# Every second ReLU of the first FFN batch on VectorE: linear attention, Fourier mixing and an FFN on one Trainium2 core

## The chip, the cores and the metric

The kernel runs on one core of one Trainium2 chip. The metric is the device time of one launch in microseconds (us), as the median of several runs. The kernel before takes 438.59 us (three runs, 438.15 to 439.4).

## The reference

Eight batches of 8 heads, 576 rows and 64 columns pass through a linear attention whose feature map has 2 x 128 features; the result, as 576 x 512 per batch, is mixed by the real part of a 2-D Fourier transform, normalised, and put through a two-layer FFN.

```python
def phi(x):
    proj = np.einsum('bhsd,df->bhsf', x, w_phi)
    proj = proj - np.max(np.abs(proj), axis=-1, keepdims=True)
    return np.concatenate([np.exp(proj), np.exp(-proj)], axis=-1)
q_p, k_p = (phi(q), phi(k))
kv = np.einsum('bhsf,bhsd->bhfd', k_p, v)
z = np.sum(k_p, axis=2)
num = np.einsum('bhsf,bhfd->bhsd', q_p, kv)
den = np.einsum('bhsf,bhf->bhs', q_p, z)[..., None] + 1e-06
attn = num / den                      # then (batch, 576, 512) = x
...
mixed = np.real(np.fft.fft(np.fft.fft(x, axis=1), axis=2))
u = x + mixed
mu = np.mean(u, axis=-1, keepdims=True)
var = np.mean((u - mu) ** 2, axis=-1, keepdims=True)
un = (u - mu) / np.sqrt(var + 1e-06)
ch = np.maximum(un @ w_ch1, 0.0) @ w_ch2       # 512 -> 2048 -> 512
out = u + ch
```

The ReLU in question is `np.maximum(..., 0.0)`, with 2048 hidden features per row.

## The kernel before

The work of a batch is split into generators, called streams, and each call of `step` runs one of them up to its next `yield`. The string `PLAN` (lines 23 to 37) is the order, written out by hand, in which the steps of all streams and batches are issued; line 1344 walks through it. A step issues its instructions to all the engines it uses, and each engine then runs its own instructions in that order. Instructions of different engines are tied together by semaphores where one needs what another made.

The streams that matter here are these:

- T, `steps` of `features` (lines 624 to 632), projects keys and queries on TensorE into PSUM tiles `psk`, `psh`, `ph` (pool `pj`, two buffers) and takes their exponentials on ScalarE: `KPp` and `KPn` (L502), `QPHP` and `QPHN` (L611, L586).
- P, `maxima`, projects the queries again into tiles `psq` and takes their row maxima on VectorE, `MQ` (L560, L538). In batches 0 and 1 each step takes two `psq` tiles from the pool `pb`.
- R, `kmax`, takes the row maxima of `psk` on VectorE, `MK` (L516). S, `scaled`, makes `VCn` and `VCp` from them, first a small exponential on ScalarE (L466), then the product on GpSimd (L471).
- M, `mixing`, first multiplies features and values (`kv`, L892 and L896, copied by ScalarE as `kvh`, L900), then combines each head (`pn_`, L992; `tg`, `cb`, `rd` on VectorE, L999 to L1006; `X` on GpSimd, L1007), then does the Fourier transform.
- N, `normalise`, subtracts the row mean (`nm` on VectorE, L1131 and L1136; `UN` on ScalarE, L1145) and, in batch 0, transposes on TensorE (`put`, L1160) with a copy to `UT` (L1164 on VectorE, L1166 on ScalarE). U, `scales`, takes the statistics on VectorE (L1175, L1176).
- F, `forward`, is the FFN. `hidden` makes 16 groups (hh = 0 to 15) of four matmuls each into a tile `psf` (L1220) and applies the ReLU to it on ScalarE into `HT` (L1224). In batch 0 it runs twice in a row, for the columns 0 to 256 and for 256 to 576, before `output` (L1231, then L1237 on VectorE) begins; each group is one step of F. Below, h0 to h15 are the groups with 256 columns and g0 to g15 those with 320.

The tiles `psf`, `psq`, `put`, `pu`, `pm`, `px` and `pso` share the pool `pb`, which has three buffers in PSUM. They are handed out in turn, so a tile's first matmul waits until the tile that was asked for three places earlier has been read out by its reader. While batch 0 is in `hidden`, the plan runs the features, maxima and `kv` of batch 1 between its groups.

Of the kernel before, what the change touches and what calls it, by code (L numbers as in the profile page):

```python
# [9 lines left out]
AT = mybir.ActivationFunctionType  # L10
# [30 lines left out]
def kernel(  # L41
# [10 lines left out]
    nc = tc.nc  # L52
# [1145 lines left out]
    def store(b, U, c):  # L1198
        if c == 1:
            for a in range(8):  # L1200
                nc.sync.dma_start(
                    out=out[b, 225 - 32 * a:257 - 32 * a, :].rearrange("(r j) n -> r j n", j=2),
                    in_=U[16 * a:16 * a + 16, 0:2, 0:C],
                )
        elif c in (2, 3):
            rows_ = out[b, 320:576, :].rearrange("(a r j) n -> a r j n", r=16, j=2)
            nc.sync.dma_start(out=rows_[:, ::-1, 3 - c, :], in_=U[:, c, 0:C])
        elif c == 4:
            nc.sync.dma_start(out=out[b, 257:320, :], in_=U[1:64, 4, 0:C])
            nc.sync.dma_start(out=out[b, 0:1, :], in_=U[0:1, 4, 0:C])  # L1210

    def forward(b):
        U, UT = turned_u[b]
        HT = fpool.tile([128, NHH, S], BF16, tag="HT", name="HT")

        def hidden(lo, hi):
            for hh in range(NHH):
                ps = pb.tile([128, hi - lo], F32, tag="pb", name="psf")
                for cc in range(NCC):
                    nc.tensor.matmul(  # L1220
                        ps[:], lhsT=W1b[:, cc, 128 * hh:128 * hh + 128], rhs=UT[:, cc, lo:hi],
                        start=(cc == 0), stop=(cc == NCC - 1),
                    )
                nc.scalar.activation(out=HT[:, hh, lo:hi], in_=ps[:], func=AT.Relu)  # L1224
                yield

        def output(c):
            at = PLACE[c]
            po = pb.tile([128, C], F32, tag="pb", name="pso")
            for hh in range(NHH):  # L1230
                nc.tensor.matmul(  # L1231
                    po[:], lhsT=HT[:, hh, at:at + 128], rhs=W2b[:, hh, :],
                    start=(hh == 0), stop=(hh == NHH - 1),
                )
                if hh % 2 and hh < NHH - 1:
                    yield
            nc.vector.scalar_tensor_tensor(  # L1237
                out=U[:, c, 0:C], in0=po[:], scalar=scale_of[b, c], in1=U[:, c, 0:C],
                op0=ALU.mult, op1=ALU.add,
            )  # L1240
            store(b, U, c)
            yield

        yield from hidden(0, 256)
        if b == 0:
            yield from hidden(256, S)
        yield from output(0)
        yield from output(2)
        if b > 0:
            yield from hidden(256, S)  # L1250
        yield from output(1)
        yield from output(3)
        po = pb.tile([128, C], F32, tag="pb", name="pso")
        for hh in range(NHH):
            g = 64 * (hh % 2)
            nc.tensor.matmul(
                po[g:g + 64, :], lhsT=HT[:, hh, 512:576], rhs=W2b[:, hh, :],
                start=(hh < 2), stop=(hh >= NHH - 2),
            )
            if hh % 4 == 3 and hh < NHH - 1:  # L1260
                yield
        for g in (0, 64):
            nc.vector.scalar_tensor_tensor(
                out=U[0:64, 4, 0:C], in0=po[g:g + 64, :], scalar=scale_of[b, 4][0:64],
                in1=U[0:64, 4, 0:C], op0=ALU.mult, op1=ALU.add,
            )
        store(b, U, 4)
        yield
# [109 lines left out]
```

## Time and profile before

The profiled execution has a span of 436.2 us; the run it was taken from gave 438.0 us. The runs without a profile have their median at 438.59 us.

| engine | busy us | share of the span |
|---|---|---|
| TensorE (PE) | 407.8 | 93% |
| VectorE (DVE) | 339.6 | 78% |
| ScalarE (ACT) | 308.3 | 71% |
| GpSimd (POOL) | 208.6 | 48% |

The granted TensorE clock is 0.99 of full speed. A busy TensorE is not one at its peak, since the ends of its matmuls are modelled. The shares are averages over the whole span. The FFN's first layer of batch 0 lies at 53 to 84 us, and there the shares are others; the tables by stretch (columns: busy us of PE, of its weight loads PEld, of DVE, of ACT, of POOL, with instruction counts; then granted clock, DMA share and GB/s) and the chain of work that ended last (columns: start us, us, what) show that part by itself.

### The profile page before, as it was taken

The page shows a single profiled execution, that of the slowest core. Times are in us where ns is not written, and L with a number is a line of the kernel's source. Part 1 is how long each engine was busy: PE and PEld are TensorE (multiplying, and loading weights), DVE is VectorE, ACT ScalarE, POOL GpSimd, SP SyncE. Part 2 cuts the span into 40 slices and gives each one's busy share as a digit, 9 for nine tenths or more (in the row PEclk, how much of TensorE's full clock was granted, in tenths as well). Part 3 has the DMA queues.
Part 4 walks back from the last instruction along what each step waited for, and adds up shares of the span by engine and source line. Part 5 has one row for each costly group of instructions (what it writes and reads, how often), then busy time and mean ns, then how long its engine had stood idle before and what let it go on. Part 6 is the DMA issues. An engine that isn't in the chain of part 4 may idle for free.

```text
span 436.2 us, 10470 instructions
## 1 busy us (share of the span) xinstructions
PE 407.8 (93%) x4110; PEld 255.4 (59%) x4110; DVE 339.6 (78%) x720; ACT 308.3 (71%) x661; POOL 208.6 (48%) x269
## 2 busy tenths in 40 slices
PE   8888898989899999999899899999999999999993
PEld 3564476643675548565666458565766467656561
DVE  6989875899959985998679985898889885965302
ACT  2986999655985798498847788588957886346350
POOL 7982568646545094636645445823652542300100
PEclk9899999999999999999999999999999999999998
DMA  8899995976469357493779467693743050104304
GB/s 223 164 204 147 158 142 60 167 88 108 85 71 141 55 99 128 82 152 54 134 88 127 43 92 100 105 143 61 128 89 59 16 109 20 26 0 77 66 23 84
DMA packets 108626, 42.70 MB, mean 98 GB/s; under 512 B 82849, under 2 KB 103457, under 8 KB 108577
## 3 DMA queue, kind: packets, MB, share of 16 engines
q0 software_dynamic: 45936, 16.60, 34.2%
q1 hardware_dynamic: 62481, 25.38, 31.0%
q8 instruction: 32, 0.52, 0.5%
q14 instruction: 17, 0.14, 0.1%
q10 hardware_dynamic: 160, 0.07, 0.1%
HBM read 36.77 MB, written 9.44 MB: 106 GB/s over the span
## 4 chain that ended last, share of the span: by engine, by line
PE 48%; DVE 28%; ACT 14%; POOL 3%; DMA 3%; issue 2%; DVEq 0%; POOLq 0%; ACTq 0%; SPq 0%
PE psf L1220 22%; PE pso L1231 12%; DVE cb L1004 4%; DVE tg L999 3%; DMA UT<-UN 3%; DVE MK L516 2%; DVE R L908 2%; DVE X L1095 2%; PE kv L892 2%; PE psD L1050 2%; ACT HT L1224 2%; DVE X L1237 2%; DVE st L1175 2%; ACT KPn L502 2%; ACT QPHN L611 1%
## 5 line engine op out<-in xcount | busy, mean ns | idle before, releaser
L1220 PE MATMUL psf<-UT,W1b 128*128 128x320 bf16 (+1 forms) x1024 | 142.2, 286 | 3.8 <-DMA UT<-UN 3.4
L1231 PE MATMUL pso<-W2b,HT 128*128 128x512 bf16 x512 | 125.7, 379 | 0.0
L1224 ACT ACTIVATE HT<-psf 128x256 bf16<-128x256 f32 (+1 forms) x256 | 100.0, 416 | 33.7 <-PE psf L1220 26.5
L1220 PEld LDWEIGHTS <-W1b 128*128 128x128 bf16 x1024 | 94.6, 98 | 35.0 <-issue 10.0
L1231 PEld LDWEIGHTS <-HT 128*128 128x128 bf16 x512 | 45.8, 98 | 44.2 <-issue 1.6
L1007 POOL TENSOR_TENSOR X<-cb,rd 128x320 f32<-128x320 f32 x56 | 41.2, 735 | 59.8 <-DVE rd L1006 44.5
L471 POOL TENSOR_TENSOR VCn<-VS,VCn 128x512 bf16<-128x512 bf16 x28 | 29.7, 1062 | 36.2 <-ACT VCn L466 30.4
L502 ACT ACTIVATE KPp<-psk 128x1024 bf16<-128x1024 f32 x28 | 28.8, 1030 | 22.3 <-PE psk L496 22.2
L560 DVE TENSOR_REDUCE MQ<-psq 128x8 f32<-128x1024 f32 (+1 forms) x32 | 34.3, 1084 | 9.3 <-PE psq L552 9.1
L1237 DVE SCALAR_TENSOR_TENSOR X<-pso,rs,X 128x512 f32<-128x512 f32 x32 | 23.6, 738 | 22.8 <-PE pso L1231 22.7
L502 ACT ACTIVATE KPn<-psk 128x1024 bf16<-128x1024 f32 x28 | 28.6, 1022 | 13.9 <-DVE MK L516 13.6
L516 DVE TENSOR_REDUCE MK<-psk 128x8 f32<-128x1024 f32 x28 | 33.9, 1212 | 0.2
L1095 DVE TENSOR_TENSOR X<-pu,X 128x512 f32<-128x512 f32 (+3 forms) x49 | 23.6, 530 | 11.8 <-PE pu L1105 11.7
L1152 ACT ACTIVATE UN<-X,nm 128x512 bf16<-128x512 f32 (+1 forms) x35 | 25.0, 724 | 10.7 <-DVE nm L1151 9.7
L456 POOL TENSOR_TENSOR V4N<-VS,V4N 64x256 bf16<-64x256 bf16 x14 | 8.9, 638 | 48.1 <-ACT V4N L452 34.5
L611 ACT ACTIVATE QPHP<-psh 128x1024 bf16<-128x1024 f32 x28 | 28.8, 1028 | 2.3 <-PE psh L602 1.9
L471 POOL TENSOR_TENSOR VCp<-VS,VCp 128x512 bf16<-128x512 bf16 x28 | 29.7, 1061 | 0.0
L611 ACT ACTIVATE QPHN<-psh 128x1024 bf16<-128x1024 f32 x28 | 28.7, 1027 | 0.0
L1175 DVE BATCH_NORM_STATS2 st<-X 128x6 f32<-128x512 f32 (+1 forms) x40 | 27.2, 680 | 0.0
L1191 POOL TENSOR_TENSOR rs<-VE,mhalf 128x5 f32<-128x5 f32 (+1 forms) x9 | 10.2, 1139 | 33.2 <-DVE VE L1190 33.2
L992 PEld LDWEIGHTS <-QPHP 128*128 128x128 bf16 x280 | 20.8, 99 | 5.6 <-DVE cb L1004 2.1
L289 POOL DMA_DIRECT2D QS<-in_q_dram x28 | 23.1, 827 | 0.0
(457 smaller groups left out, 803.0 us busy)
## 6 DMA issues: line engine op xcount, KB each, us to landing
out_dram<-X SPq DMA_DIRECT2D x16, 256.0 KB
out_dram<-X SPq DMA_DIRECT2D x64, 64.0 KB
KS<-in_k_dram POOLq DMA_DIRECT2D x7, 512.0 KB, 7.6
QS<-in_q_dram POOLq DMA_DIRECT2D x14, 256.0 KB, 8.0
VS<-in_v_dram POOLq DMA_DIRECT2D x14, 256.0 KB, 6.1
W1b<-in_moe_w_ch_dram POOLq DMA_DIRECT2D x1, 2048.0 KB, 18.9
W2b<-in_moe_w_ch_dram POOLq DMA_DIRECT2D x1, 2048.0 KB, 15.4
W2b<-in_k_dram SPq DMA_DIRECT2D x2, 512.0 KB
```

The lines of the kernel that those rows point to most:

```text
L471: nc.gpsimd.tensor_tensor(out=VC[:, hs, :, 0:D], in0=values[b][0][:, hs, :].rearrange("p h (j d) -> p h j d", d=D), in1=VC[:, hs, :, D:D + ...
L502: nc.scalar.activation(out=KP[:, hs, :, :].rearrange("p e (jp jj) f -> p jj (e jp) f", jj=2), in_=psk[:], func=AT.Exp, scale=sgn,)
L516: nc.vector.tensor_reduce(out=MK[:, 2 * pr:2 * pr + 2, :].rearrange("p e (jp jj) -> p jj (e jp)", jj=2), in_=tiles[pr][:], axis=AX.X, op=A ...
L560: nc.vector.tensor_reduce(out=o, in_=i[:], axis=AX.X, op=ALU.max, apply_absolute_value=True)
L611: nc.scalar.activation(out=o, in_=psh[:], func=AT.Exp, scale=sgn)
L1007: nc.gpsimd.tensor_tensor(out=X[:, :, D * h:D * h + D], in0=cb[:, :, 0:D], in1=rd[:].to_broadcast([128, 5, D]), op=ALU.mult,)
L1095: nc.vector.tensor_tensor(out=to, in0=more, in1=to, op=ALU.add)
L1175: nc.vector.bn_stats(out=st[0:M, :], in_=X[0:M, c, 0:C])
L1220: nc.tensor.matmul(ps[:], lhsT=W1b[:, cc, 128 * hh:128 * hh + 128], rhs=UT[:, cc, lo:hi], start=(cc == 0), stop=(cc == NCC - 1),)
L1224: nc.scalar.activation(out=HT[:, hh, lo:hi], in_=ps[:], func=AT.Relu)
L1231: nc.tensor.matmul(po[:], lhsT=HT[:, hh, at:at + 128], rhs=W2b[:, hh, :], start=(hh == 0), stop=(hh == NHH - 1),)
L1237: nc.vector.scalar_tensor_tensor(out=U[:, c, 0:C], in0=po[:], scalar=scale_of[b, c], in1=U[:, c, 0:C], op0=ALU.mult, op1=ALU.add,)
```

## The change

In batch 0, the groups with odd hh have their ReLU done by VectorE, as a maximum with 0, in place of ScalarE. This concerns h1, h3, ... h15 and g1, g3, ... g15, 16 of the 32 ReLUs of batch 0. The other batches, the matmuls and the plan are as before. Each moved instruction keeps its place in the order of issue, between what the plan issues before and after it to the engine that it now runs on. Lines after the edit are numbered three higher: the ScalarE ReLU becomes L1227, the VectorE one is L1225.

```diff
@@ hidden @@
-                nc.scalar.activation(out=HT[:, hh, lo:hi], in_=ps[:], func=AT.Relu)
+                if b == 0 and hh % 2:
+                    nc.vector.tensor_scalar_max(out=HT[:, hh, lo:hi], in0=ps[:], scalar1=0.0)
+                else:
+                    nc.scalar.activation(out=HT[:, hh, lo:hi], in_=ps[:], func=AT.Relu)
                 yield
```

## The prediction

> **What bounds the kernel now.** The ReLUs of batch 0 lie in one stretch, so I read the chain of waits for that stretch first (start us, us, what).
>
> ```profile
> 53.94 0.72 ACT UN L1145
> 54.66 0.82 ACT HT L1224 x3
> 55.48 0.51 ACT UT L1166
> ...
> 73.67 0.33 ACT HT L1224
> 74.00 0.17 ACT kvh L900
> 74.17 0.04 issue
> 74.21 0.62 PE pt L568 x4
> ...
> 78.06 0.33 PE pn__1491 L992 x10
> 78.39 0.02 issue
> 78.41 0.51 DVE tg L999
> ...
> 83.87 0.57 DVE R L908
> ```
>
> From 53.94 to 74.17 every link is on ACT. Then PE leads for 4 us, and from 78.41 DVE leads; the chain of the next stretch stays on DVE until 104.56. So the 32 ReLUs fall into three parts: 16 (h) and six (g0 to g5) on an ACT-bound path, four (g6 to g9) around the PE part, and the last six in a DVE-bound part. How full each engine is comes from the stretches:
>
> ```profile
> 58.00:62.00 4.00, 3.76 (x59) 3.00 (x58) 3.85 (x8) 4.00 (x10) 4.00 (x6) 1.00 1.07 123
> 62.00:66.00 4.00, 3.75 (x51) 2.66 (x45) 3.17 (x6) 4.00 (x11) 1.54 (x2) 1.00 0.84 87
> ...
> 78.00:82.00 4.00, 4.00 (x59) 2.96 (x57) 3.24 (x10) 3.16 (x8) 3.20 (x4) 1.00 1.55 161
> ```
>
> ACT is at 4.00 of 4.00, but DVE (the third count) is not free: 3.85 of 4 at 58 to 62. What room DVE has is in its timeline, where the idle time before an instruction stands in brackets:
>
> ```profile
> 58.08 0.68 DVE L1090 SCALAR_TENSOR_TENSOR X<-pu,X 64x512 f32<-64x512 f32 x1 [1.20 <-PE pu L1105]
> 62.38 1.29 DVE L560 TENSOR_REDUCE MQ<-psq 128x4 f32<-128x512 f32 x2 [0.42 <-PE psq L552]
> 67.84 1.28 DVE L538 TENSOR_REDUCE MQ<-psq 64x4 f32<-64x512 f32 x2 [0.52 <-PE psq L532]
> 76.55 0.50 DVE L999 TENSOR_TENSOR tg<-pn__1450,E 128x325 f32<-128x325 f32 x1 [3.78 <-ACT HT L1224]
> 78.41 0.50 DVE L999 TENSOR_TENSOR tg<-pn__1491,E 128x325 f32<-128x325 f32 x1 [0.56 <-PE pn__1491 L992]
> ```
>
> With 0.31 and 0.35 in two rows not shown, DVE is idle for 1.20 + 0.42 + 0.31 + 0.52 + 0.35 + 3.78 + 0.56 = 7.14 us up to 83.87, and over half of that is one gap at 72.8 to 76.55, late in the stretch.
>
> **What the Trainium skill says.** "VectorE: DVE Perf Modes", section "Why PSUM operands drop a tier": an fp32 operand in PSUM leaves VectorE at one element a cycle. The trace agrees: the bf16 copy of 320 fp32 elements out of PSUM took 491 ns, 512 elements from SBUF only 486 ns.
>
> ```profile
> L1056 DVE CAST DT<-psD 128x320 bf16<-128x320 f32 x1 | 0.5, 491 | 1.8 <-ACT DT L1055 1.8
> L1140 DVE TENSOR_SCALAR UN<-X,nm 128x512 bf16<-128x512 f32 x1 | 0.5, 486 | 0.0
> ```
>
> "PSUM — Partial Sum Buffer", section "Engine vs sequencer instructions": the queues of ScalarE and VectorE are strictly first in, first out, so a waiting ReLU holds everything behind it. In the trace each engine's instructions start in program order. The same page, "PSUM bank collisions raise a hardware error": two engines may not touch one bank at once, so readers of one tile are ordered. That fits L516 and L502, which both only read `psk`: ACT waited for DVE there ten times, 13.6 us. Hence a late `MK` can hold ACT and the reverse.
>
> **The change part by part.**
>
> *Off ACT.* Back to back, a 256-column ReLU takes 0.27 us of the chain (three took 0.82) and a 320-column one 0.33. Up to 74.17, eight of the first and three of the second go: 8 x 0.27 + 3 x 0.33 = 3.2 us of ACT work. That is the most this part can give.
>
> *On DVE.* The trace has no ReLU on DVE. Nearest is the L1056 copy, 0.49 us for 320 elements; with the 512-element copy of L380 at 0.685 us the slope is 0.194 / 192 = 1.0 ns an element, so 256 elements come to 0.43. Instructions in a row overlap by 0.08 to 0.09 us (two L560 of 0.68 took 1.28), so the queue pays 0.34 and 0.40: 8 x 0.34 + 8 x 0.40 = 5.9 us. The skill's price (the first page, section "The TRN2 errata — SBUF-src ops pay a fixed extra latency per instruction", 120 cycles plus one per element at 0.96 GHz) gives 0.39 and 0.46, 0.03 us less each, so 5.4 us with the same overlap. I take 5.9 and keep 5.4 as the lower end.
>
> *The two together.* If every idle moment of DVE could be used, DVE would reach its instruction of 83.87 by 7.14 - 5.9 = 1.2 us sooner (1.7 with the lower price). The room bounds the gain at 1.2 to 1.7 us, whatever ACT saves.
>
> *What it reaches in order.* I followed the queues by hand from 53 us, with durations and waits of the trace, the DVE ReLUs at their new places and the three `pb` buffers handed out as before. From PE to the reader I count 0.04 us (the tenth 320-column group ended at 78.92, its ReLU began at 78.96), from the reader's visible end to PE 0.03 (ReLU end 54.95, `put` 54.98). The delays against before:
> - h1 stands between the two `MK` of 52.80; its matmuls end at 54.07, so it costs 0.16 of wait and 0.34. h3 stands behind the second `MK`, 0.30 before its matmuls end at 55.86, and costs 0.30 and 0.34. All that follows on DVE is 1.15 late, `nm` too, on which ACT's `UN` (56.65) waits: ACT, two ReLUs lighter, starts it 0.60 late.
> - The wait of 1.20 before 58.08 takes up most of h5 and of that delay; X is 0.2 late, h7 follows, and the `MQ` pair of 59.54 starts at 60.1 (+0.55). Its two tiles are the buffers that h9 and h10 wait for, so PE comes 0.5 late to h10, the next `kv` and `psk`, and ACT's KPp of 62.16 starts at 62.7.
> - h9 precedes the next `MK` and `MQ`; h11 and h13 the `MK` of 64.41. h13's matmuls end at 65.3, and this `MK` ends at 66.9, not 65.6. ACT's VCn (65.85 in the chain), which reads it, starts at 66.95 (+1.1), though ACT has done seven ReLUs fewer by then; it idles.
> - h15 and g1 come before the L538 pair (67.84), which starts at 69.3 (+1.4); g3 keeps this. Its tiles hold up g2 and g3 on PE, and through `psq` and `kv` ACT's QPHN of 69.58 (+1.2).
> - g5 lies in the 3.78 gap and costs DVE nothing, and ACT is a ReLU shorter: `kvh` of 73.78, `pt` of 74.21 and `tg` of 76.55 come 1.1 late.
> - g7 is ready behind the first `rd` and fills the 0.56 wait in part; with g9 behind it the second `tg` is 1.27 late. g11, g13, g15 lie in the DVE-bound part and add 3 x 0.40 = 1.2: R of 83.87 is 2.5 late.
>
> From there the chain is DVE's to 104.56 and no second path is shortened, so 2.5 us go to the end. Against the profiled span: 436.2 + 2.5 = 438.7; the runs without a profile have their median at 438.59, 2.4 above that span, so 438.59 + 2.5 = 441.1 us. The matmuls, DMA issues and GpSimd's work are neither more nor fewer and keep their order.
>
> **The rivals.** A change within 0.3% (1.3 us) can't be told from none here.
> 1. *ACT's relief wins.* For it: ACT is full for 20 us and leads the chain, and PE was held by it (put at 54.98, `pt` at 74.21). If the waits that I place in front of h3, h9 and h13 close up because PE and ACT both run earlier, DVE's idle time is used and the room decides: 438.59 - 1.2 to 1.7 = 436.9 to 437.4. Against it: over half of the room is one gap at 72.8, which ReLUs queued before it fill only by being late.
> 2. *No difference.* The first part gains or loses under 1 us where I have a loss of 1.1, and the 1.4 us behind 76.55 takes the gain away: -1.0 + 1.4 = +0.4, 439.0 us. For it: my path has many links, each good to about 0.05 us.
> 3. *Pile-up.* The idle time doesn't take up any ReLU, as each of them waits for PE behind a maximum that PE's next buffer waits for: 438.59 + 5.9 = 444.5 at the most; half-way from my forecast, 442.8. Against it: the gap at 72.8 hides at least g5.
>
> **How the numbers follow.** My forecast, 441.1 us with its own range 439.9 to 442.6, has 0.5; no difference (437.3 to 439.9) 0.27; ACT's relief 0.12, of which the part over 0.3% needs the lower price too; pile-up 0.11. Slower is forecast and pile-up, 0.61; within 0.3% 0.27; faster 0.12, rounded up for what my path may have wrong in sign. The range of 437.6 to 443.2 leaves out about one in ten on either side.
>
> **What would show it.** Right: L1225 in 16 rows at 0.43 and 0.49 us, with idle time in front of several ascribed to `psf`; ACT below full at 62 to 74; VCn of 65.85 and the L538 of 67.84 later by about 1; the first `tg` after 76.55 and R of 83.87 later by 1 and 2.5; from there the same distance to the end. Wrong: the first `tg` before 76; or ReLUs at under 0.35 us; or a delay at 84 that is smaller at the end. If L516 and L560 keep their old times up to 68, the coupling through the three buffers is what I have wrong.

## The result and the profile after

The changed kernel takes 443.32 us (median of four runs, 442.36 to 444.64) where the kernel before takes 438.47 beside it: 4.85 us more, a ratio of 1.0106 with a 95% interval of 1.0066 to 1.0146. The forecast was 441.1, so the sign was right, the loss was about twice the 2.5 us that I had worked out, and the time lies 0.1 us beyond the upper end of the range.

The profiled execution has a span of 440.5 us, 4.3 more than before. As the clearest measure of the stretch I take the time on VectorE from the first of the two `MK` maxima ahead of the ReLUs (L516, at 52.80 before) to the start of `R` (L908, at 83.78 in the timeline of before; the chain, which puts a start where the instruction ahead has ended, says 83.87). It was 83.78 - 52.80 = 30.98 us. In the timeline of VectorE of the changed kernel (start us, us, instruction, idle time in front in brackets) it is 88.01 - 52.00 = 36.01, 5.03 us more:

```profile
52.00 1.21 DVE L516 TENSOR_REDUCE MK<-psk 128x8 f32<-128x1024 f32 x1
...
55.56 1.07 DVE L234 TENSOR_SCALAR TURN<-gs,blk 128x128 f32<-128x128 f32 x1
56.55 0.14 DVE L230 TENSOR_SCALAR blk<-pc_i 128x1 f32<-128x1 int32 x1
56.73 0.92 DVE L234 TENSOR_SCALAR TURN<-gs,blk 128x128 f32<-128x128 f32 x1
57.57 0.20 DVE L1131 TENSOR_SCALAR nm<-sm 128x1 f32<-128x1 f32 x1
...
62.67 0.42 DVE L1225 TENSOR_SCALAR HT<-psf 128x256 bf16<-128x256 f32 x1 [0.80 <-PE psf L1220]
...
79.44 0.50 DVE L999 TENSOR_TENSOR tg<-pn__1450,E 128x325 f32<-128x325 f32 x1 [2.47 <-ACT HT L1227]
...
88.01 1.67 DVE L908 TENSOR_TENSOR R<-X 128x512 f32<-128x512 f32 x2
```

This execution reached the stretch 0.80 us sooner than the one before (52.00 and 52.80). The two run together up to 15.2 us and are 0.68 us apart at an `MK` maximum (L843, at 22.42 and 23.10); between these points TensorE's granted clock is 0.55 and 0.59 in before (16 to 18 and 18 to 20 us), and 1.00 in the changed kernel. From `R` to the end the two are alike: 440.5 - 88.0 = 352.5 and 436.2 - 83.8 = 352.4. So the loss arises in the stretch, and 5.03 - 0.80 + 0.1 = 4.3 is the difference of the spans.

Two things in it were not in my working. The first is TURN, two tables of 128 x 128 numbers that VectorE makes once in this stretch (L234), and that nothing reads before the `pt` matmuls (L568, at 74.21 in before). Its two instructions took 1.07 and 0.92 us; before, they took 0.29 each (first fence below, VectorE of before). What differs is what GpSimd does meanwhile (second and third fence, GpSimd of before and of after):

```profile
55.27 0.29 DVE L234 TENSOR_SCALAR TURN<-gs,blk 128x128 f32<-128x128 f32 x1
...
55.65 0.29 DVE L234 TENSOR_SCALAR TURN<-gs,blk 128x128 f32<-128x128 f32 x1
```

```profile
53.81 0.62 POOL L456 TENSOR_TENSOR V4P<-VS,V4P 64x256 bf16<-64x256 bf16 x1
56.57 1.06 POOL L471 TENSOR_TENSOR VCn<-VS,VCn 128x512 bf16<-128x512 bf16 x1 [2.13 <-issue]
```

```profile
55.49 1.06 POOL L471 TENSOR_TENSOR VCn<-VS,VCn 128x512 bf16<-128x512 bf16 x1 [1.85 <-issue]
56.51 1.06 POOL L471 TENSOR_TENSOR VCp<-VS,VCp 128x512 bf16<-128x512 bf16 x1
```

Before, TURN ran while GpSimd was idle (54.4 to 56.57). After, h1 and h3 hold it back, and it starts at 55.56, just behind the start of VCn at 55.49. Both sides moved: counted from the first L516, TURN starts 1.09 us later (3.56 for 2.47), and VCn 0.28 sooner (3.49 for 3.77), as ScalarE, without h1, comes sooner to the exponential that it needs (L466). Each TURN ends 0.08 us behind the product that it started beside (56.63 and 56.55, 57.65 and 57.57). The Trainium skill's page "SBUF — State Buffer", section "Who interferes with whom", says that VectorE in its two-port modes and GpSimd share a pair of ports, and that the one that issues first keeps the other out for the whole instruction. The rows above agree with that, as far as they go: that TURN runs in such a mode is not shown. It took 0.78 + 0.63 = 1.41 us more than before.

The second thing is TensorE's clock (stretches of the changed kernel; columns as in the prediction, the clock is the third number from the right):

```profile
57.20:59.20 2.00, 0.95 (x8) 0.63 (x8) 1.97 (x6) 1.39 (x3) 2.00 (x4) 1.00 1.22 196
59.20:61.20 2.00, 1.56 (x22) 1.23 (x22) 1.97 (x8) 2.00 (x4) 1.99 (x3) 0.76 1.17 95
61.20:63.20 2.00, 2.00 (x11) 1.44 (x10) 1.20 (x4) 1.00 (x3) 1.27 (x2) 0.50 1.26 119
63.20:65.20 2.00, 1.82 (x32) 1.39 (x31) 1.72 (x3) 1.56 (x3) 0.00 (x0) 0.89 0.31 46
```

Before, the clock was 1.00 through 50 to 64 us. Here it falls to 0.50, some 2 us behind a stretch in which PE waited for buffers (busy 0.95 of 2.00). The matmuls of h8 to h10 are drawn out (2.75 us for 1.68), ScalarE is at 1.00 of 2.00, and h9's ReLU waits 0.80 us for them. Such a drop is not new: the profile of before has one at 16 to 20 us, ahead of the stretch.

The ReLUs themselves cost what I took, 0.41 to 0.43 us for 256 columns and 0.45 to 0.49 for 320 (the answer for L1225, min/median/max in ns):

```profile
L1225 DVE TENSOR_SCALAR HT<-psf x16: 408/438/492, 53.4 to 87.6; 128x256 bf16<-128x256 f32 x8, 128x320 bf16<-128x320 f32 x8
```

### The profile page after: what moved, and what is told of

Its sections match the earlier page's. It is cut to its first block, busy times and chain, and to the rows that moved or that the text cites. A ratio compares the mean times of both kernels' runs of the same rounds, so it can differ in the third digit from the quotient of the medians.

```text
span 440.5 us, 10444 instructions
## 1 busy us (share of the span) xinstructions
PE 406.3 (92%) x4080; PEld 255.9 (58%) x4110; DVE 346.9 (79%) x736; ACT 304.5 (69%) x645; POOL 208.8 (47%) x269
## 4 chain that ended last, share of the span: by engine, by line
PE 50%; DVE 33%; ACT 10%; DMA 3%; issue 2%; POOL 1%; DVEq 0%; ACTq 0%; POOLq 0%; SPq 0%
PE psf L1220 22%; PE pso L1234 11%; DVE cb L1004 4%; DVE tg L999 3%; DMA UT<-UN 3%; DVE MK L516 3%; PE idle L1312 2%; PE kv L892 2%; DVE X L1095 2%; DVE st L1175 2%; DVE R L908 2%; PE psD L1050 2%; DVE X L1240 2%; DVE MQ L560 2%; DVE rd L1006 1%
## 5 line engine op out<-in xcount | busy, mean ns | idle before, releaser
L1234 PE MATMUL pso<-W2b,HT 128*128 128x512 bf16 x482 | 121.7, 379 | 1.6 <-issue 0.5
L1227 ACT ACTIVATE HT<-psf 128x256 bf16<-128x256 f32 (+1 forms) x240 | 93.9, 413 | 35.9 <-PE psf L1220 28.8
L516 DVE TENSOR_REDUCE MK<-psk 128x8 f32<-128x1024 f32 x28 | 33.9, 1212 | 0.0
```

The lines of the kernel that those rows point to most:

```text
L516: nc.vector.tensor_reduce(out=MK[:, 2 * pr:2 * pr + 2, :].rearrange("p e (jp jj) -> p jj (e jp)", jj=2), in_=tiles[pr][:], axis=AX.X, op=A ...
L1234: nc.tensor.matmul(po[:], lhsT=HT[:, hh, at:at + 128], rhs=W2b[:, hh, :], start=(hh == 0), stop=(hh == NHH - 1),)
```

## The experiments

The theory after the result: three parts, namely the queue order of the forecast, the collision of TURN with GpSimd, and the clock. Its first rival is plain load: each ReLU adds its 0.34 or 0.40 us to VectorE's queue, and the late TURN fills a wait that would be there anyway. "Stretch" below is the time from the first L516 to L908 as above, of the profiled execution; medians are compared with runs of the kernel before on the same chip.

**TURN issued sooner, ahead of the ReLUs' stretch.** `PLAN` is a string; its 137th letter, a C, is the step that issues TURN.

```diff
+PLAN = PLAN[:109] + "C" + PLAN[109:136] + PLAN[137:]
```

With all 16 ReLUs on VectorE:

> The changed kernel, with the two TURN instructions (L234) issued 9 us sooner, into DVE's idle time at 46 us. Theory (a chain of three parts: the late TURN meets GpSimd's products and takes 1.4 us more, PE then idles for its buffers, its clock drops to half and costs about 1 us more; the rest is queue order): 441.0 us (440.3 to 441.8), TURN at 0.29 us each, PE clock 1.00 at 57 to 66. Rival 1, plain load (each ReLU on DVE costs its 0.34 or 0.40, the collision only fills a wait that would be there anyway): 442.7 or more. Rival 2, the clock drops for PE waits that have nothing to do with TURN: 442, with the clock still at 0.5 to 0.8 at about 60 to 64.

And the same move in the kernel before:

> The kernel before with the same move of TURN alone, as control: all theories 438.5 us (within 0.5), since the two instructions lie beside ACT's path in both places. If it gains over 1 us, part of what turn_early gains is not the collision.

Measured: 441.42 us with the ReLUs moved (before: 437.87; ratio 1.0088, 1.0062 to 1.0113), and 438.93 without (ratio 1.0029, 1.0016 to 1.0042). TURN took 0.29 us each, and the stretch is 87.85 - 54.35 = 33.50 us, 2.52 over before and 2.51 under the changed kernel. But the control lost 1.06 us where I expected none, though its stretch is 30.96, as before. TURN did not land in the idle time that I aimed at: it went behind `DT` and ahead of an `MK` maximum (L511) at 48 us. And in the profile of turn_early the clock fell at 50 to 55 us (0.65 to 54), for the most part ahead of the stretch. The move has a cost of its own, which no profile here places, so the pair supports the theory without measuring the collision cleanly; turn_first below does that.

**One half of the ReLUs at a time.**

```diff
-                if b == 0 and hh % 2:
+                if b == 0 and lo == 0 and hh % 2:    # h_only
+                if b == 0 and lo > 0 and hh % 2:     # g_only
```

> Only h1, h3, ... h15 on DVE. Theory: the TURN collision, the clock drop and the waits in front of h3 to h13 all lie here, so nearly the whole delay of the first tg stays (3.7 us later in the changed kernel): 442.0 us (441.2 to 442.7). Plain load: 8 x 0.34 = 2.7 at the most, less what ACT saves and the idle time hides: 440.5 or less.

> Only g1, g3, ... g15 on DVE. Theory: g1, g3 and g5 relieve ACT while DVE waits (0.3 to 1.0 us sooner at the first tg), g7 and g9 are half hidden, g11, g13, g15 cost 0.40 each in the DVE-bound part: 438.9 us (438.2 to 439.8). Plain load: 8 x 0.40 = 3.2, of which the 3.78 gap hides g5: 440.5 or more.

Measured: h_only 442.00 us (ratio 1.0107, 1.0089 to 1.0126), g_only 438.94 (ratio 1.0027, 1.0011 to 1.0043). Plain load doesn't fit this pair: the eight shorter ReLUs, 2.7 us of work, cost 4.1, and the eight longer ones, 3.2 us of work, cost 1.1. The stretches are 33.77 and 32.07 us, 2.79 and 1.09 over before. The 4.1 holds more than the ReLUs: the five runs of h_only have a mean granted clock of 0.990, the 24 of before beside them 0.995, and among these 24 the runs at 0.991 or 0.992 took 438.5 (median), those at 0.997 or 0.998 took 437.3. From this I estimate that about 1 us of the 4.1 is the clock's. So h_only alone doesn't exclude plain load; g_only and the runs below do. In g_only the first `tg` comes 0.24 us sooner than before, counted from L516 (77.09 - 53.58 = 23.51 and 76.55 - 52.80 = 23.75), the second 0.07 sooner, and `R` 1.09 later: g11, g13 and g15 add 1.16, 0.39 each. In h_only TURN took 1.07 and 0.92 as in the changed kernel, while the clock stayed at 1.00 through the stretch.

**The changed kernel again, and with PE kept busy.** The second kernel has idle matmuls in front of h7, where PE waits for a buffer. They write to a tile that nothing reads.

```diff
+                if b == 0 and lo == 0 and hh == 7:
+                    idle = pk.tile([128, 512], F32, tag="pk", name="idle")
+                    for x in range(4):
+                        nc.tensor.matmul(
+                            idle[:], lhsT=ones_b[:],
+                            rhs=ones_b[:].unsqueeze(1).to_broadcast([128, 4, 128]),
+                            start=True, stop=True,
+                        )
                 ps = pb.tile([128, hi - lo], F32, tag="pb", name="psf")
```

> The changed kernel once more, beside the other three, for a common footing: 442.5 to 443.5 us. TURN (L234) takes about 1 us for each of its two instructions as before (collision with GpSimd's products, fixed by the order), while the half clock at 59 to 64 us may or may not come again: if it does not, this execution should be about 1.2 us shorter from the first L516 at 52 us to R (L908) than the first profile's 36.0 us.

> The changed kernel with four idle matmuls of 512 columns ahead of h7, where PE waits for a buffer (0.97 us in the changed kernel's profile). Theory that this gap lets the clock fall: the clock stays at 1.00 through 66 us and the time falls by about 1 us, to 442. Rival, that the drop comes by chance of the moment and in some executions alone: no change within 0.6 us against the changed kernel beside it.

Measured: 443.06 us for both (442.59 to 444.35 and 442.43 to 443.66; before 438.51; ratios 1.0102, 1.0081 to 1.0124, and 1.0106, 1.0086 to 1.0125). In the profiles the half clock is there without the idle matmuls and gone with them. The first fence shows stretches of after_again, the second the same of after_warm:

```profile
60.00:62.00 2.00, 1.47 (x22) 1.06 (x21) 1.93 (x7) 2.00 (x4) 1.99 (x4) 0.93 1.18 101
62.00:64.00 2.00, 2.00 (x16) 1.46 (x14) 1.32 (x4) 1.61 (x4) 1.91 (x2) 0.50 0.91 81
64.00:66.00 2.00, 2.00 (x33) 1.58 (x31) 1.60 (x3) 0.92 (x3) 0.00 (x0) 0.72 0.75 91
```

```profile
60.00:62.00 2.00, 1.46 (x23) 0.97 (x21) 1.97 (x6) 2.00 (x5) 1.99 (x4) 1.00 1.30 137
62.00:64.00 2.00, 1.79 (x24) 1.32 (x21) 1.88 (x7) 1.71 (x4) 2.00 (x2) 1.00 0.94 66
64.00:66.00 2.00, 1.76 (x34) 1.37 (x33) 2.00 (x3) 1.80 (x4) 0.04 (x1) 1.00 0.99 116
```

The stretch of after_again is 36.01 us again, that of after_warm 34.92: in the profiled executions the half clock goes with 1.09 us. The medians don't show this. The expected 1 us didn't come, and the span of after_warm's profile, 441.8, is only 0.7 below that of after_again, 442.5.

More can be read from the runs. In after_warm's profile the clock falls elsewhere, to 0.88, 0.50 and 0.77 at 214 to 220 us, and the mean granted clock of its four runs is 0.992, the same as that of the four runs of after_again. Nor is it shown that the idle matmuls held the clock up at 60 to 66: h_only has none, its PE waits for the same buffers and is as little busy there, and its clock stays at 1.00 too. The first fence is after_again, the second h_only:

```profile
58.00:60.00 2.00, 1.03 (x12) 0.69 (x8) 1.97 (x6) 0.75 (x2) 2.00 (x3) 1.00 1.21 199
```

```profile
58.00:60.00 2.00, 1.03 (x12) 0.70 (x8) 1.97 (x6) 0.76 (x2) 2.00 (x3) 1.00 1.22 201
60.00:62.00 2.00, 1.47 (x25) 1.07 (x24) 1.93 (x8) 2.00 (x4) 2.00 (x4) 1.00 1.21 110
62.00:64.00 2.00, 1.53 (x16) 1.07 (x13) 1.91 (x6) 1.56 (x4) 1.90 (x2) 1.00 1.00 79
```

h_only agrees on the price of the drop: its second `tg` comes 28.40 us behind the first L516, that of after_warm 28.39, that of after_again 29.47.

**h1 and h3 apart from the rest.**

```diff
-                if b == 0 and hh % 2:
+                if b == 0 and hh % 2 and (lo > 0 or hh > 3):    # from_h5
+                if b == 0 and lo == 0 and hh in (1, 3):         # h1_h3_only
```

> The changed kernel with h1 and h3 back on ScalarE, 14 of 16 moved. Theory (the collision of TURN needs h1 and h3 ahead of it): TURN at 0.29 us each and nm in time; left are the queue order of h7 to h15 (about 0.9 us) and the g part (1.0 us, as g_only shows): 440.2 us (439.5 to 440.9). Plain load: 2 x 0.34 less than the changed kernel, 442.5.

> Only h1 and h3 on DVE. Theory: the queue wait (1.1 us) and the collision (1.4 us) make nm late by 2.5, of which ACT, two ReLUs lighter, passes on about 1.9 us to the first tg and to the end: 440.2 us (439.4 to 440.8), two ReLUs doing nearly half of the whole harm. Plain load: 2 x 0.34 us at the most, 438.7 or less.

Measured: from_h5 441.53 us (ratio 1.0069, 1.0053 to 1.0085), 1.53 below the changed kernel beside it; h1_h3_only 440.09 (ratio 1.0037, 1.0013 to 1.0061), 1.58 above before. Two ReLUs of 0.34 us thus cost 1.5 us or more, and taking them off the 16 gives back as much; plain load allows 0.7. In from_h5 TURN is at 0.29 each, and its stretch is 33.53 us, 2.55 over before. My 440.2 for it was too low by 1.3: with 1.09 of the 2.55 from the g part, h5 to h15 cost 1.46 in the queue and not 0.9. In h1_h3_only TURN took 1.07 and 0.92, and the profiled execution had the half clock at 60 to 66 us (0.77, 0.50, 0.87). It is also the longest of its seven, 441.45 us, at a mean clock of 0.989; the other six lie between 439.29 and 440.43, at 0.991 to 0.997, which suggests that the drop comes in some executions and not in all.

**TURN ahead of h3, all 16 moved.**

```diff
+PLAN = PLAN[:133] + "C" + PLAN[133:136] + PLAN[137:]
```

> The changed kernel, all 16 ReLUs on DVE, with the TURN pair issued three steps sooner, ahead of h3 in DVE's queue, so that it begins before GpSimd's VCn product. Theory (collision): TURN at 0.29 us each, nm 1.4 us sooner, from the first L516 to R (L908) 33.5 us, or 34.0 as h3 comes 0.7 later, in place of 36.0: 441.3 us (440.5 to 442.0) with the kernel before at 438.5. Rival (the late TURN fills a wait that other instructions keep): 443 as in the changed kernel. If the clock still falls to half at 60 to 66 us, about 1 us more, in either case.

Measured: 441.26 us (before 438.40; ratio 1.0063, 1.0043 to 1.0084). VectorE and GpSimd of this kernel:

```profile
52.90 1.22 DVE L517 TENSOR_REDUCE MK<-psk 128x8 f32<-128x1024 f32 x1
...
55.92 0.29 DVE L235 TENSOR_SCALAR TURN<-gs,blk 128x128 f32<-128x128 f32 x1
56.12 0.15 DVE L231 TENSOR_SCALAR blk<-pc_i 128x1 f32<-128x1 int32 x1
56.30 0.29 DVE L235 TENSOR_SCALAR TURN<-gs,blk 128x128 f32<-128x128 f32 x1
56.51 0.42 DVE L1226 TENSOR_SCALAR HT<-psf 128x256 bf16<-128x256 f32 x1
...
86.56 1.68 DVE L909 TENSOR_TENSOR R<-X 128x512 f32<-128x512 f32 x2
```

```profile
56.39 1.12 POOL L472 TENSOR_TENSOR VCn<-VS,VCn 128x512 bf16<-128x512 bf16 x1 [1.86 <-issue]
```

The second TURN starts at 56.30, 0.09 ahead of VCn, and keeps its 0.29; now it is VCn that is a little longer, 1.12 for 1.06. The stretch is 33.66 us, 2.68 over before, and the clock was 1.00 at 50 to 94. The ReLUs are the same 16 with the same matmuls, and only the place of TURN, three steps sooner, differs: the loss is 2.9 us in place of 4.6 and 4.9, the two measurements of the changed kernel. Their mean granted clocks are alike, 0.992 to 0.993. So the place of TURN is worth 1.7 to 2.0 us in the medians; against after_warm, which has the full clock too, it is 34.92 - 33.66 = 1.26 us in the stretch.

**Only the ReLUs with room.**

```diff
-                if b == 0 and hh % 2:
+                if b == 0 and hh in ((1, 3, 5) if lo else (5, 6)):
```

> Only h5, h6, g1, g3 and g5 on DVE, where the kernel before leaves DVE waiting. Theory (what counts is the place in DVE's queue): TURN untouched, no ReLU in front of a maximum that PE's buffers wait for, except g1 and g3, which cost nothing in g_only; ACT sheds 2 x 0.27 + 3 x 0.33 = 1.5 us, a third of it reaches the end as in g_only (0.24 of 1.0): 0.2 to 0.8 us faster than before, 438.0 with 438.5 before. Plain load: 2 x 0.34 + 3 x 0.40 = 1.9 more on DVE, no gain: 438.5 to 440.4.

Measured: 438.73 us (before 438.40; ratio 1.0005, 0.9990 to 1.0019), no difference that can be told, and not the gain I expected. VectorE waits 0.76 us for h5's matmuls; the first `tg` comes 0.08 sooner from L516 and the stretch is 30.91 us, 0.07 less. The 1.5 us taken off ScalarE don't come through: some turn into waits of ScalarE for matmuls (0.17, 0.17, 0.22 and 0.21 us up to 73 us), and where the rest stays was not followed. No version that I tried beats the kernel before.

## Why the prediction came out as it did

**The sign was right, and nothing contradicts the bound.** I had put the room of VectorE at 7.1 us, of which ReLUs fill 5.9, so that a gain of 1.2 to 1.7 was the most. None of the ten other versions and repeats is faster than before, not even slack_five, which takes only ReLUs with room; so the bound was never tested.

**The queue order was right, to a few tenths.** turn_first is the changed kernel without the collision, from_h5 without h1 and h3 as well, and both profiles have the full clock in the stretch. Their stretches are 2.68 and 2.55 us longer than before, the forecast said 2.5, and their times are 2.9 and 3.0 longer. That the two are so near each other shows that h1 and h3 by themselves cost little: as forecast, the wait of 1.20 takes up most of their delay (the `X` of 58.08 is 0.14 late in turn_first). The links can be set side by side, each counted from the first L516, as delay against before:

| link | forecast | turn_first | changed kernel |
|---|---|---|---|
| `nm` of 55.85 | 1.15 | 0.89 | 2.52 |
| `MQ` pair of 59.54 | 0.55 | 0.48 | 1.86 |
| L538 pair of 67.84 | 1.4 | 1.67 | 4.02 |
| first `tg`, 76.55 | 1.1 | 1.34 | 3.69 |
| second `tg`, 78.41 | 1.27 | 1.52 | 3.86 |
| `R` | 2.5 | 2.68 | 5.03 |

For turn_first the times are 56.84, 60.12, 69.61, 77.99, 80.03 and 86.56, less 52.90; for the changed kernel 57.57, 60.60, 71.06, 79.44, 81.47 and 88.01, less 52.00. `nm` of turn_first comes sooner than forecast, as TURN no longer waits behind h3.

**The step that failed is the first of the path**, "All that follows on DVE is 1.15 late, `nm` too". I moved TURN by 1.15 us and kept its duration of 0.29. The shift itself was right (1.09 measured), but it put TURN beside VCn, and the two TURN took 1.41 us more: `nm` is 2.52 late, nearly 1.15 + 1.41. I wrote that GpSimd's work keeps its order, which is true of its own queue, and looked neither at when VCn would start nor at what stands beside VectorE's moved instructions. ScalarE's `UN`, for which I had 0.60, waited 1.95 us for `nm` and started 1.96 late (57.81 - 52.00 and 56.65 - 52.80), and the chain of the changed kernel (start us, us, what) goes through both TURN:

```profile
55.04 0.42 DVE HT L1225
...
55.56 1.07 DVE TURN L234
...
56.73 0.92 DVE TURN L234
57.65 0.12 DVE nm L1131
57.77 0.33 DVE HT L1225
```

The profile of before had a hint of this. The same instruction, L735, appears there twice with 284 and 1335 ns. The longer one starts just behind the start of a GpSimd product (VectorE, then GpSimd, of before); the shorter one starts beside a product too, but only 0.24 us ahead of its end (23.44 + 1.05 = 24.49):

```profile
24.25 0.28 DVE L735 CAST m<-MQ 128x20 bf16<-128x20 f32 x1
...
28.94 1.33 DVE L735 CAST m<-MQ 128x20 bf16<-128x20 f32 x1
```

```profile
28.90 1.06 POOL L874 TENSOR_TENSOR VCp<-HT,VCp 128x512 bf16<-128x512 f32 x1
```

**The sum.** By the stretches of the profiles: the g part 1.09 (g_only), the queue of h5 to h15 1.46 (from_h5 less g_only), h1, h3 and the collision 1.39 (after_warm less from_h5), the half clock 1.09 (after_again less after_warm). These are differences along one chain, so they make 5.03 by construction; a test from outside it is h_only, whose 2.79 with the g part of 1.09 makes 3.88, where after_warm has 3.94. That the third is the collision and not the two ReLUs' own time is shown by turn_first, which has them and costs only 0.13 more than from_h5. The first three are also in the medians: 1.1 for g_only, 1.9 for from_h5 less g_only, each by its own runs of before (3.0 - 1.1), and 1.5 for the third, together the 4.55 of after_again. The fourth isn't, and it is no part of what the change adds to an ordinary run as far as the mean clock tells: that is 0.993 and 0.992 in the two sets of four runs of the changed kernel, and 0.993 in the runs of before beside after_again.

**What I left out and can't settle** is where the clock falls. Two profiles of the changed kernel have the half clock at the same place, one of h1_h3_only as well, h_only, turn_first and from_h5 don't, and turn_early has it earlier, at 50 to 55. Eleven of the twelve profiles, that of before among them, have 4 us or more of it somewhere ahead of the last 10 us. With the idle matmuls it was gone from its place in one profile, but no time from the median. The Trainium skill's page "TensorE: Matmul & The Clock Gate", Part 1, says that the array's clock is halved until it has been busy for a while, and again after a window of idling. The half clock does stand behind PE's waits, but the longest of them in the changed kernel is 0.97 us, and behind the same waits it came in after_again and not in h_only. Likewise PE is busy for 1.05 and 1.06 of 2 us at 14 to 16 us in before and in the changed kernel, and only before has the half clock behind that. What decides between them no run here shows.

**The rivals.** ACT's relief did happen, but small: 0.24 us at the first `tg` in g_only. Pile-up, at 442.8 the nearest in time to 443.3, was right in little but its number: the gap at 72.8 did hide g5, and what came on top of the forecast came for the most part from an instruction that isn't a ReLU.

## What to carry to other kernels

When an edit shifts a queue, look at what the shifted instructions will stand beside on the other engines, not only at what waits behind them; here two instructions of 0.29 us grew to 1.07 and 0.92 us by starting 0.07 and 0.22 us behind the start of a GpSimd product. An instruction that a profile lists with two durations far apart is a sign to look for, and issuing it a few steps sooner undid that part here. ReLUs handed to an engine that is idle for 22% of the span helped nowhere: most of its idle time lay elsewhere than the ReLUs, the maxima behind them held the PSUM buffers that PE needed next, and even the five that fell into idle time brought 0.07 us of the stretch and nothing in the median. And before a drop of the clock in a profile is put down to a change, look whether the profile of the kernel before has one in another place.

## What was not expected of the hardware

- A VectorE `tensor_scalar` of 128 fp32 elements from SBUF took 0.29 us by itself and 1.07 or 0.92 us beside a GpSimd product of 1.06; started 0.09 us ahead of the product it kept its 0.29.
- TensorE's granted clock fell to 0.50 for about 3 us behind a stretch of 2 us in which PE was busy for 0.95, with less waiting than I would have thought enough; in another execution with the same waits it stayed at 1.00. With such a drop the stretch was 1.09 us longer; the profile of before, with a drop at 16 to 20 us, fell 0.68 us behind one without it between 15 and 23 us.
